# Two gated MLPs behind an attention block: longer buffers for the low parts of split operands

## Chip, cores, metric

One core of one Trainium2 chip. The metric is the device time of one launch in microseconds (us); the kernel before takes 986.37 us, the median of three runs (985.73 to 987.92).

## What is computed

```python
def _attn_ref(x, inducing):                       # x 1 x 12480 x 128, inducing 32 x 128
    h = mab(I, x)                                 # 32 inducing points attend to all rows
    return mab(x, h)                              # every row attends to the 32 results

def _moe_ref(x, w_in, w_out, alpha):              # w_in 128 x 2048, w_out 2048 x 128
    h = x @ w_in
    g = np.maximum(h, 0.0) + alpha * np.minimum(h, 0.0)
    return (g @ w_out).astype(np.float32)

def _moe2_ref(x, w_in, w_out):
    h = np.maximum(x @ w_in, 0.0)
    return (h * h @ w_out).astype(np.float32)
...
    x = attn_out.reshape(B * S, D)
    x = _moe_ref(x=x, **moe_kwargs)
    return _moe2_ref(x=x, **moe2_kwargs)
```

Rows: 12,480, cut into 30 row tiles of T = 416. The hidden width of 2,048 is cut into 16 chunks of 128.

## The kernel before

A first stage (some 100 us) loads and transposes x, runs the first attention, and brings the weights into shape. Then comes the main loop, a software pipeline over 480 chunk indices (30 row tiles x 16 chunks), written out step by step at the end of the function (lines 725 to 739).

Precision is kept by splitting: a float32 operand is stored as a high part in the reduced type float32r and a low part, the remainder, in the same type. A product then takes three matmuls with the same output bank (`three`, line 586): high by the weight's high part (L587), high by the weight's low part (L588), low by the weight's high part (L589). The parts are the moving operands, 128 partitions x 416 elements of 4 bytes, 1,664 bytes a partition.

In step s PE gets ten matmuls, in this order:
- L577 (`l1_a`, chunk s): `a_s`, the attention weights of the row tile s div 16, by `w1s`. ACT makes `g1h` of it (L581), DVE `g1l` (L583).
- L587, L588, L589 (`l2_a`, chunk s - 24): `y1h`, `y1h`, `y1l` by the second MLP's input weights w2i. ACT makes `r` (L619), DVE its square `sq` (L621), ACT `g2h` (L627), POOL `g2l` (L629).
- the same lines (`l1_b`, chunk s - 3): `g1h`, `g1h`, `g1l` by wo, summed into `y`.
- the same lines (`l2_b`, chunk s - 28): `g2h`, `g2h`, `g2l` by w2o, summed into `y`.

Where s - 3 is a multiple of 16, `l2_b` comes before `l1_b`. After the 16th chunk of a row tile `l1_b` calls `end_y1`: one more matmul (L604, `a_s` by `v_s`), then `y1h` (ACT, L606) and `y1l` (DVE, L608). Every fourth row tile four small matmuls for the next attention scores (L436) come in between. In the first 24 steps and the last 28 parts of the step are missing. PE works in program order; each other engine works through its own queue, and semaphores say when a tile may be read or overwritten.

Each kind of tile has a ring of buffers, taken in turn: `g1h`, `g1l`, `g2h`, `g2l` four each, `y1h`, `y1l` two each, `a_s` five. The buffers of a ring lie one behind the other in SBUF. As 1,664 is 6.5 x 256, neighbours in a ring begin at two offsets within 256 bytes in turn:

```
ring    first buffer at byte   start within 256 bytes, and who has which
g1h     170432                 192, 64, 192, 64   main loop: chunk even 192, odd 64
g1l     177088                 192, 64, 192, 64   main loop: chunk even 192, odd 64
g2h     183744                 192, 64, 192, 64   chunk even 192, odd 64
g2l     190400                 192, 64, 192, 64   chunk even 192, odd 64
y1h     197056                 192, 64            row tile even 192, odd 64
y1l     200384                 192, 64            row tile even 192, odd 64
a_s     131648                 64, 192, 64, 192, 64   row tile mod 5 is 2 or 4: 192, else 64
```

The weights' blocks all begin at 160 within 256 bytes (`v_s` at 32). As g1 has chunk s - 3 and g2 chunk s - 28, an even step has g1 at 64 and g2 at 192, an odd step g1 at 192 and g2 at 64. (For the first 20 chunks g1 uses the rings of g1 and g2 in turn.) In the trace, step 256 begins at 520.67 us, step 264 at 535.96, step 272 at 550.95, step 280 at 566.14 and step 288 at 581.13. Steps 256 to 271 have `a_s` of row tile 16 (at 64), steps 272 to 287 of row tile 17 (at 192); steps 248 to 263 have y1 of row tile 14 (at 192), steps 264 to 279 of row tile 15 (at 64), steps 280 to 295 of row tile 16 (at 192).

Of the kernel before, what the change touches and what calls it, by code (L numbers as in the profile page):

```python
# [10 lines left out]
F32R = mybir.dt.float32r  # L11
# [7 lines left out]
T = 416  # L19
# [9 lines left out]
def attention_then_two_mlps(ctx: ExitStack, tc, x, inducing, w_in, w_out, alpha, w2_in, w2_out, out):  # L29
# [7 lines left out]
    P = 128  # L37
# [531 lines left out]
    wk = ctx.enter_context(tc.tile_pool(name="wk", bufs=1))  # L569
# [3 lines left out]
    def l1_a(i, other_bank):  # L573
        t, c = divmod(i, NCH)
        b = h2_bank() if other_bank else h1_bank()
        a = a_s[t]
        nc.tensor.matmul(b[:, :T], w1s[: a.shape[0], c * P : (c + 1) * P], a, start=True, stop=True)  # L577

        tag = "g2" if i < EARLY and i % 2 else "g1"
        hi = wk.tile([P, T], F32R, name="g1h", tag=tag + "h", bufs=4)  # L580
        nc.scalar.activation(hi, b[:, :T], AF.Relu)  # L581
        lo = wk.tile([P, T], F32R, name="g1l", tag=tag + "l", bufs=4)
        nc.vector.scalar_tensor_tensor(lo, b[:, :T], 0.0, f32(hi), op0=ALU.max, op1=ALU.subtract)  # L583
        g1[i] = hi, lo

# [5 lines left out]
    def l1_b(i):  # L591
        t, c = divmod(i, NCH)
        if c == 0:
            y1_cur[t] = y1_bank() if t != 1 else y2_bank()
        b = y1_cur[t][:, :T]
        hi, lo = g1.pop(i)
        three(b, wo_hi[:, c, :], wo_lo[:, c, :], hi, lo, c == 0, False)
        if c == NCH - 1 and t:
            end_y1(t)

    def end_y1(t):
        b = y1_cur.pop(t)[:, :T]
        a = a_s.pop(t)
        nc.tensor.matmul(b, v_s[: a.shape[0]], a, start=False, stop=True)  # L604
        hi = wk.tile([P, T], F32R, name="y1h", tag="y1h", bufs=2)
        nc.scalar.copy(hi, b)  # L606
        lo = wk.tile([P, T], F32R, name="y1l", tag="y1l", bufs=2)
        nc.vector.tensor_tensor(lo, b, f32(hi), op=ALU.subtract)  # L608
        y1_split[t] = hi, lo

# [13 lines left out]
    def l2_split(i):  # L624
        sq = rr.pop(i)
        hi = wk.tile([P, T], F32R, name="g2h", tag="g2h", bufs=4)
        nc.scalar.copy(hi, sq)  # L627
        lo = wk.tile([P, T], F32R, name="g2l", tag="g2l", bufs=4)
        (nc.vector if i >= total - LAG2 else nc.gpsimd).tensor_tensor(lo, sq, f32(hi), op=ALU.subtract)  # L629
        g2[i] = hi, lo  # L630

# [54 lines left out]
    at(19, copy_u)  # L686
    at(20, step_v)
    at(22, end_y1, 0)
    for tiles in groups[1:]:
        for k, v in enumerate(second_attention(tiles)):  # L690
# [34 lines left out]
    for s in range(total + LAG2 + LAG2B + 4):  # L725
        if s < total:
            l1_a(s, s < LAG2 and s % 2)
        if 0 <= s - LAG2 < total:
            l2_a(s - LAG2)
        if 0 <= s - LAG2 - 1 < total:  # L730
            l2_split(s - LAG2 - 1)

        ends = [(l1_b, i) for i in l1_b_at.get(s, [])]
        if 0 <= s - LAG2 - LAG2B < total:
            ends.insert(0 if ends and ends[0][1] % NCH == 0 else len(ends), (l2_b, s - LAG2 - LAG2B))
        for f, i in ends:
            f(i)
        for f in plan.pop(s, []):
            f()
# [30 lines left out]
```

## Time and profile before

| | |
|---|---|
| runs | 987.92, 985.73, 986.37 us; median 986.37 |
| the profiled execution | 985.42 us, its span 983.6 us, 1.8 us lie around the span |
| mean granted TensorE clock | 0.997 |
| busy: PE, PE's weight loads, ACT, DVE, POOL | 965.0, 936.8, 768.5, 683.1, 555.1 us |
| instructions: PE, ACT, DVE, POOL | 5341, 1600, 1203, 518 |

A matmul's duration runs from its start to its modelled end and covers more than its turn on the array: the matmuls overlap, and the next one starts some 187 ns after the one before. The time that a step takes is read from the starts of the same line in consecutive steps; the timeline gives them to 0.01 us.

### The profile page before, as it was taken

What the parts mean: (1) busy time and instruction counts of PE and PEld (TensorE: products, weight loads), DVE (VectorE), ACT (ScalarE), POOL (GpSimd) and SP (SyncE); (2) the same over time, 40 slices, a digit from 0 to 9 for tenths busy, and PEclk for the clock granted to TensorE, in tenths of its full rate; (3) what the DMA queues carried; (4) which work ended last, traced back from release to release, by engine and by line L of the source; (5) the groups of instructions that cost most, each with busy time, mean ns of one, the idle gap of its engine ahead of it and who ended that gap; (6) DMA issues with size and microseconds to landing.
All of it is one profiled execution on the core that took longest, in us unless ns stands there. A gap on an engine that the chain in (4) does not pass through costs nothing.

```text
span 983.6 us, 16078 instructions
## 1 busy us (share of the span) xinstructions
PE 965.0 (98%) x5341; PEld 936.8 (95%) x5341; DVE 683.1 (69%) x1203; ACT 768.5 (78%) x1600; POOL 555.1 (56%) x518
## 2 busy tenths in 40 slices
PE   8889999999999999999999999999999999999997
PEld 6578999999999999999999999999999999999997
DVE  5788876667766677666776667766677666766677
ACT  5789887778877777777787777877778777787776
POOL 2358765555655556555565555655556555565530
PEclk9999999999999999999999999999999999999999
DMA  9431001000010000100001000010001000010001
GB/s 329 147 101 55 10 11 34 10 10 10 15 30 10 10 9 18 27 10 10 10 21 25 10 9 10 23 23 10 9 9 30 16 10 10 10 27 1 10 9 19
DMA packets 66356, 28.42 MB, mean 29 GB/s; under 512 B 54224, under 2 KB 62176, under 8 KB 66272
## 3 DMA queue, kind: packets, MB, share of 16 engines
q1 hardware_dynamic: 66272, 27.39, 11.3%
q8 instruction: 42, 0.69, 0.3%
q14 instruction: 42, 0.34, 0.1%
HBM read 14.80 MB, written 6.39 MB: 22 GB/s over the span
## 4 chain that ended last, share of the span: by engine, by line
PE 94%; DVE 2%; ACT 2%; DMA 1%; issue 0%; POOL 0%; SPq 0%; ACTq 0%; DVEq 0%
PE y L589 18%; PE y L588 18%; PE y L587 18%; PE h L587 9%; PE h L589 9%; PE h L588 9%; PE h L577 9%; PE h L248 1%; PE ms L260 1%; PE ms L436 1%; PE y L604 1%; ACT g1h L581 1%; PE y L321 1%; DMA xg<-in_x_dram 0%; DVE g1l L583 0%
## 5 line engine op out<-in xcount | busy, mean ns | idle before, releaser
L629 POOL TENSOR_TENSOR g2l<-sq,g2h 128x416 fp32r<-128x416 f32 x456 | 495.9, 1088 | 343.9 <-ACT g2h L627 244.2
L583 DVE SCALAR_TENSOR_TENSOR g1l<-h,g1h 128x416 fp32r<-128x416 f32 x480 | 282.7, 590 | 220.9 <-ACT g1h L581 216.5
L581 ACT ACTIVATE g1h<-h 128x416 fp32r<-128x416 f32 x480 | 248.7, 519 | 131.6 <-PE h L577 128.6
L621 DVE TENSOR_TENSOR sq<-h,r 128x416 f32<-128x416 f32 x480 | 283.6, 591 | 52.3 <-ACT r L619 4.9
L619 ACT ACTIVATE r<-h 128x416 f32<-128x416 f32 x480 | 249.4, 520 | 53.9 <-PE h L589 8.5
L627 ACT CAST g2h<-sq 128x416 fp32r<-128x416 f32 x480 | 255.4, 532 | 3.2 <-DVE sq L621 3.1
L577 PE MATMUL h<-a_s,w1s 128*128 128x416 f32 (+1 forms) x480 | 170.0, 355 | 4.5 <-DVE g1l L583 2.8
L589 PE MATMUL y<-g2l,w2o_hi 128*128 128x416 f32 x480 | 168.7, 351 | 0.3 <-POOL g2l L629 0.3
L587 PE MATMUL h<-y1h,w2i_hi 128*128 128x416 f32 x480 | 168.2, 350 | 0.2
L589 PE MATMUL y<-g1l,wo_hi 128*128 128x416 f32 x480 | 168.3, 351 | 0.0
L589 PE MATMUL h<-y1l,w2i_hi 128*128 128x416 f32 x480 | 167.9, 350 | 0.2 <-DVE y1l L608 0.2
L588 PE MATMUL h<-y1h,w2i_lo 128*128 128x416 f32 x480 | 168.0, 350 | 0.0
L588 PE MATMUL y<-g2h,w2o_lo 128*128 128x416 f32 x480 | 167.8, 350 | 0.0
L588 PE MATMUL y<-g1h,wo_lo 128*128 128x416 f32 x480 | 167.8, 350 | 0.0
L587 PE MATMUL y<-g1h,wo_hi 128*128 128x416 f32 x480 | 167.5, 349 | 0.0
L587 PE MATMUL y<-g2h,w2o_hi 128*128 128x416 f32 x480 | 167.5, 349 | 0.0
L577 PEld LDWEIGHTS h<-a_s,w1s 128*128 128x128 f32 (+1 forms) x480 | 90.1, 188 | 12.5 <-DVE g1l L583 6.1
L587 PEld LDWEIGHTS h<-y1h,w2i_hi 128*128 128x128 f32 x480 | 90.0, 188 | 3.1 <-DVE sq L621 1.7
L587 PEld LDWEIGHTS y<-g1h,wo_hi 128*128 128x128 f32 x480 | 90.3, 188 | 1.0 <-issue 0.5
L589 PEld LDWEIGHTS y<-g2l,w2o_hi 128*128 128x128 f32 x480 | 90.1, 188 | 1.2 <-POOL g2l L629 0.7
L589 PEld LDWEIGHTS h<-y1l,w2i_hi 128*128 128x128 f32 x480 | 90.0, 188 | 0.7 <-DVE y1l L608 0.5
L588 PEld LDWEIGHTS y<-g1h,wo_lo 128*128 128x128 f32 x480 | 90.2, 188 | 0.4
(121 smaller groups left out, 749.8 us busy)
## 6 DMA issues: line engine op xcount, KB each, us to landing
out_dram<-o SPq DMA_DIRECT2D x120, 52.0 KB, 1.9
xg<-in_x_dram SPq DMA_DIRECT2D x10, 512.0 KB, 8.4
raw<-in_moe_w_in_dram SPq DMA_DIRECT2D x8, 512.0 KB, 6.4
raw<-in_moe_w_out_dram SPq DMA_DIRECT2D x8, 512.0 KB, 4.1
a_s<-a_hi SPq DMA_DIRECT2D x58, 52.0 KB, 1.9
a_s<-a_lo SPq DMA_DIRECT2D x58, 52.0 KB, 1.9
xg<-in_x_dram SPq DMA_DIRECT2D x4, 256.0 KB, 3.8
xg<-in_x_dram SPq DMA_DIRECT2D x1, 96.0 KB, 5.8
```

The lines of the kernel that those rows point to most:

```text
L248: nc.tensor.transpose(b[:, k * p : (k + 1) * p], x_t[g][:p, i, k, :], ident[:p, :p])
L260: nc.tensor.matmul(b[i * M : (i + 1) * M, :n], indT, xT[:, t0 : t0 + n], start=True, stop=True, tile_position=(0, i * M),)
L577: nc.tensor.matmul(b[:, :T], w1s[: a.shape[0], c * P : (c + 1) * P], a, start=True, stop=True)
L581: nc.scalar.activation(hi, b[:, :T], AF.Relu)
L583: nc.vector.scalar_tensor_tensor(lo, b[:, :T], 0.0, f32(hi), op0=ALU.max, op1=ALU.subtract)
L587: nc.tensor.matmul(b, w_hi, hi, start=start, stop=False)
L588: nc.tensor.matmul(b, w_lo, hi, start=False, stop=False)
L589: nc.tensor.matmul(b, w_hi, lo, start=False, stop=stop)
L619: nc.scalar.activation(r, b, AF.Relu)
L621: nc.vector.tensor_tensor(sq, b, r, op=ALU.mult)
L627: nc.scalar.copy(hi, sq)
L629: (nc.vector if i >= total - LAG2 else nc.gpsimd).tensor_tensor(lo, sq, f32(hi), op=ALU.subtract)
```

## The change

The three rings of low parts get tiles that are 32 elements longer, of which the first 416 are used. A buffer is then 1,792 = 7 x 256 bytes long, and all buffers of `g1l`, `g2l` and `y1l` begin 192 bytes past a multiple of 256. The rings of four grow by 512 bytes, that of two by 256; what lies behind them moves by 512, 1,024 or 1,280 bytes. All other tiles keep their offset within 256 bytes, the high parts and `a_s` with the two offsets in turn among them. The last buffer ends at byte 216,640 of a partition (215,360 before).

```diff
@@ -579,7 +579,7 @@
         hi = wk.tile([P, T], F32R, name="g1h", tag=tag + "h", bufs=4)
         nc.scalar.activation(hi, b[:, :T], AF.Relu)
-        lo = wk.tile([P, T], F32R, name="g1l", tag=tag + "l", bufs=4)
+        lo = wk.tile([P, T + 32], F32R, name="g1l", tag=tag + "l", bufs=4)[:, :T]
         nc.vector.scalar_tensor_tensor(lo, b[:, :T], 0.0, f32(hi), op0=ALU.max, op1=ALU.subtract)
@@ -604,7 +604,7 @@
         hi = wk.tile([P, T], F32R, name="y1h", tag="y1h", bufs=2)
         nc.scalar.copy(hi, b)
-        lo = wk.tile([P, T], F32R, name="y1l", tag="y1l", bufs=2)
+        lo = wk.tile([P, T + 32], F32R, name="y1l", tag="y1l", bufs=2)[:, :T]
         nc.vector.tensor_tensor(lo, b, f32(hi), op=ALU.subtract)
@@ -625,7 +625,7 @@
         hi = wk.tile([P, T], F32R, name="g2h", tag="g2h", bufs=4)
         nc.scalar.copy(hi, sq)
-        lo = wk.tile([P, T], F32R, name="g2l", tag="g2l", bufs=4)
+        lo = wk.tile([P, T + 32], F32R, name="g2l", tag="g2l", bufs=4)[:, :T]
         (nc.vector if i >= total - LAG2 else nc.gpsimd).tensor_tensor(lo, sq, f32(hi), op=ALU.subtract)
```

## Rows read from the trace of the kernel before

**Rows 1.** The page: busy time and share of the engines, and the chain by engine.
```profile
PE 965.0 (98%) x5341; PEld 936.8 (95%) x5341; DVE 683.1 (69%) x1203; ACT 768.5 (78%) x1600; POOL 555.1 (56%) x518
...
PE 94%; DVE 2%; ACT 2%; DMA 1%; issue 0%; POOL 0%; SPq 0%; ACTq 0%; DVEq 0%
```

**Rows 2.** Windows: stretch, length, busy of PE, PEld, DVE, ACT, POOL, clock, DMA.
```profile
300.00:500.00 200.00, 200.00 (x1073) 197.32 (x1072) 137.16 (x237) 157.22 (x325) 116.53 (x108) 1.00 0.07 13
```

**Rows 3.** Groups by line, 300 to 500 us: count, busy, mean ns, idle before.
```profile
L629 POOL TENSOR_TENSOR g2l<-sq,g2h 128x416 fp32r<-128x416 f32 x105 | 114.0, 1086 | 82.9 <-ACT g2h L627 59.3 <-PE y L589 23.6
...
L583 DVE SCALAR_TENSOR_TENSOR g1l<-h,g1h 128x416 fp32r<-128x416 f32 x105 | 62.0, 590 | 50.7 <-ACT g1h L581 49.5
```

**Rows 4.** Timeline of PE, 520 to 582 us: start, duration (us); L577 begins a step.
```profile
520.67 0.35 PE L577 MATMUL h<-a_s,w1s 128*128 128x416 f32 x1
...
524.41 0.35 PE L577 MATMUL h<-a_s,w1s 128*128 128x416 f32 x1
...
525.73 0.35 PE L604 MATMUL y<-a_s,v_s 128*128 128x416 f32 x1
...
526.50 0.35 PE L577 MATMUL h<-a_s,w1s 128*128 128x416 f32 x1
...
532.21 0.35 PE L577 MATMUL h<-a_s,w1s 128*128 128x416 f32 x1
...
535.96 0.35 PE L577 MATMUL h<-a_s,w1s 128*128 128x416 f32 x1
...
537.83 0.35 PE L577 MATMUL h<-a_s,w1s 128*128 128x416 f32 x1
...
539.71 0.35 PE L577 MATMUL h<-a_s,w1s 128*128 128x416 f32 x1
...
541.57 0.35 PE L577 MATMUL h<-a_s,w1s 128*128 128x416 f32 x1
...
543.45 0.35 PE L577 MATMUL h<-a_s,w1s 128*128 128x416 f32 x1
...
545.32 0.35 PE L577 MATMUL h<-a_s,w1s 128*128 128x416 f32 x1
...
547.20 0.35 PE L577 MATMUL h<-a_s,w1s 128*128 128x416 f32 x1
...
549.07 0.35 PE L577 MATMUL h<-a_s,w1s 128*128 128x416 f32 x1
...
550.95 0.35 PE L577 MATMUL h<-a_s,w1s 128*128 128x416 f32 x1
...
566.14 0.35 PE L577 MATMUL h<-a_s,w1s 128*128 128x416 f32 x1
...
581.13 0.35 PE L577 MATMUL h<-a_s,w1s 128*128 128x416 f32 x1
```

**Rows 5.** PE's groups by line in the odd step 265, 537.81 to 539.69 us.
```profile
L588 PE MATMUL h<-y1h,w2i_lo 128*128 128x416 f32 x1 | 0.4, 353 | 0.0
L587 PE MATMUL h<-y1h,w2i_hi 128*128 128x416 f32 x1 | 0.3, 350 | 0.0
...
L577 PE MATMUL h<-a_s,w1s 128*128 128x416 f32 x1 | 0.3, 348 | 0.0
L589 PE MATMUL h<-y1l,w2i_hi 128*128 128x416 f32 x1 | 0.3, 348 | 0.0
```

**Rows 6.** PE's groups by line in the even step 282, 569.88 to 571.75 us.
```profile
L589 PE MATMUL y<-g1l,wo_hi 128*128 128x416 f32 x1 | 0.4, 353 | 0.0
L588 PE MATMUL y<-g1h,wo_lo 128*128 128x416 f32 x1 | 0.3, 350 | 0.0
L577 PE MATMUL h<-a_s,w1s 128*128 128x416 f32 x1 | 0.3, 349 | 0.0
```

**Rows 7.** PE's groups by line in the even step 264, 535.94 to 537.81 us.
```profile
L589 PE MATMUL y<-g1l,wo_hi 128*128 128x416 f32 x1 | 0.3, 347 | 0.0
```

**Rows 8.** PE's groups by line in step 260, 528.38 to 530.29 us.
```profile
L587 PE MATMUL y<-g2h,w2o_hi 128*128 128x416 f32 x1 | 0.4, 355 | 0.0
```

## The prediction

> **What bounds the kernel.** I read the page's busy shares and its chain first: TensorE (PE) is busy for 98% of the 983.6 us and makes 94% of the chain that ended last [rows 1]. The windows by stage say where: in the stretch from 300 to 500 us PE is busy for all 200.00 us at a granted clock of 1.00, which is the 2.4 GHz level [rows 2]. So in the main loop nothing but the distance from one matmul's start to the next sets the time. The writers of the low parts are far from that: in those 200 us POOL works 114.0 us on `g2l` and is idle 82.9 us ahead of it, DVE 62.0 us on `g1l` with 50.7 us idle [rows 3].
>
> The starts of L577, one per step of ten matmuls, show that steps are not equally long. From 535.96 to 550.95 us even and odd steps alternate: the four even ones take 7.47 us together (1.8675 each), the four odd ones 7.52 us (1.880 each). From 566.14 to 581.13 us eight steps take 14.99 us, 1.874 each, and so do the two from 520.67 to 524.41 us, 1.87 each [rows 4].
>
> **Which matmuls slip.** The mark is the duration. In an odd step of the first stretch `a_s`, `y1h` by w2i_hi and `y1h` by w2i_lo take 348, 350 and 353 ns, and `y1l` after them 348 [rows 5]. In a step of the second stretch it is `g1h` by wo_lo and `g1l` that show 350 and 353 ns, and `a_s` has the plain 349 [rows 6]. In the even steps of the first stretch `g1l` shows 347 [rows 7]. Laid beside the table of offsets, this has one reading. In the first stretch `a_s` and all y1 tiles lie at 64 (buffers of row tiles 16 and 15). An odd step then runs 64 64 64 64 | 192 192 192 | 64 64 64, and slips at its third tile and at its tenth, the third 64 after each change from 192. The even step after it begins inside a run of 64s that has paid already, and its first seven tiles cost nothing more. In the second stretch `a_s` and y1 lie at 192, and each step has one run of three 64s (g1 in even steps, g2 in odd ones): one slip. Around 520 us `a_s` is at 64 and y1 at 192; a single 64 between 192s adds nothing to 1.87 us. So **a run of moving operands at 64 pays once, at its third tile, whether that is a low tile or a high one**. The price: two slips make 1.880 out of 1.8675, one slip 1.874 (14.99/8), so 6.3 ns by either.
>
> **The change part by part.** Nothing is added or removed on any queue: no instruction, DMA or wait. Ten buffers grow by 128 bytes. Later tiles move by 512, 1,024 or 1,280 bytes, all multiples of 256, and keep their offsets; their first use lies behind the first stage's last reads as before, price nothing. The writers of the lows write at 192 in every step instead of every second; both offsets are in the means of [rows 3], and the idle time there covers a difference. Without that cover a longer write would show as PE waiting for `g1l` or `g2l`.
>
> What is left is the order of offsets in PE's 4,830 matmuls of the main loop, laid out from the code (480 steps of ten, and 30 of L604). Before: 82 runs of one 64, none of two, 519 of three or more (255 of three, 123 of four, 141 of six to eleven). After, with all lows at 192: 162 of one, **583 of two** (the highs of one triple), 138 of three or more (136 are `a_s` and two `y1h`, all at 64).
> - Removed: 519 x 6.3 ns = 3.27 us.
> - Kept: 138 x 6.3 ns = 0.87 us.
> - New: 583 x the price of a run of two, which the trace doesn't show. Lower bound 0, as for the run of one [rows 4]; a gain below the no-slip step is excluded because no context gives a step under 1.8675. Upper bound 6.3 ns, the full slip, 3.67 us. I take 1 ns, because the nearest row is the second tile of a longer run, 350 ns where 349 is plain [rows 5, 6], and the tile that paid the rest will no longer be at 64. That is 0.58 us.
>
> Sum: -3.27 + 0.87 + 0.58 = **-1.82 us**. The profiled execution took 985.42 us, so 983.60; the median of the runs shown is 986.37, 0.95 above it, and there the change gives **984.55 us**, 0.18% less. A measurement of this kernel tells about 0.2% (1.97 us) from no change, so the forecast lies just inside. Own range of this case: with 0 and with 2.5 ns for a run of two it is 984.0 to 985.4; about 0.9 us lower still if the disturbed steps below vanish.
>
> **Rivals.**
> *A. A run of two pays the whole slip.* Place: the second `g1h` and `g2h` matmul of each step, and `y1h` where it is at 64. For it: a slip may be owed from the entry and only show two tiles later. Against: the run of one owes nothing. Price 583 x 6.3 = 3.67 us, net +1.27 us, **987.6 us**. It decides above 4.1 ns per run, where 583 runs eat the 2.40 us.
>
> *B. A disturbed state lasts, slower than before.* From 526.50 to 532.21 us three steps take 5.71 us, 1.903 each, 30 ns over their neighbours [rows 4], and in them nearly every matmul is long, up to 355 ns for `g2h` at 192 [rows 8]. It begins behind L604, which ends a row tile, and where `a_s` is at 64 and y1 at 192 it lasts for three steps; I count 29 such steps, 0.9 us. What ends it is a step with a run of four 64s, and the change takes those runs away there. If it then lasts through all steps of that context (3/10 of 480, 144), that costs 144 x 30 ns = 4.3 us, 3.4 more than now: -1.82 + 3.4 = +1.6, **988.0 us**; if it spreads to half of all steps, 990.9. It decides from some 90 disturbed steps on. For it: after the change offsets alternate more often everywhere. Against: single 64s elsewhere don't start it.
>
> *C. Only the lows' offset counts.* Every slip goes, with the disturbed steps: -3.27 - 0.9, **982.2 us**; with the disturbed steps left, 983.1. Against: in [rows 5] the 353 ns stand at a high tile.
>
> *D. The change doesn't touch what makes the slips*, for instance PSUM banks or weights of odd chunks, which alternate with the same parity: 986.4 us. Against: which matmul slips changes with the buffers of `a_s` and y1 at the same parity [rows 5, 6]. The Trainium skill's page "SBUF — State Buffer" (SBUF: two separate sides) would stand behind this rival: it says that engines conflict only at the port pair that VectorE and GpSimd share and that TensorE waits for nobody, so an address could not matter; by it the sum is 0. The trace does not agree: steps with the same instructions differ by 13 ns with the offsets alone.
>
> **Numbers.** Chances: forecast 0.45 (nearly half of it beyond 0.2%, by the cheap end of a run of two or the vanished disturbed steps), A 0.2, B 0.17, C 0.1, D 0.08. Faster by over 0.2%: two fifths to half of the forecast's 0.45, plus C and a little for slips that I read too small, 0.34. Slower by over 0.2%: most of B and the top of A, 0.17. Within: 0.49. The range reaches from 983.0 (C with the disturbed steps left) to 988.4 (A, and B in its one context); B spread further and the low end of C are left out.
>
> **What would show it.** Right: steps with `a_s` and y1 at 192 (and those with only one of them at 64) fall from 1.874 to about 1.869 us; with both at 64 each step shows 1.874, its 353 ns at `y1h` by w2i_lo in even and odd steps; the whole-run means of `g1l` and `g2l` fall to 349 ns, while that of `y1h` by w2i_lo does not fall. A: the steps show 1.880, with long durations at or behind the second `g1h` and `g2h`. B: many steps at 1.90. Wrong altogether: slips that keep their places, or PE idle ahead of L587 to L589 behind DVE or POOL.

## The result, and the profile after

The changed kernel takes 999.98 us (median of 4 runs, 998.36 to 1001.33) against 986.15 us; the ratio is 1.0138 (95% interval 1.0123 to 1.0153). That is 13.8 us slower, outside the range forecast. All times here and below are of executions with a mean granted clock of 0.94 or more; two executions of `all64` (clock 0.557 and 0.752) and one of `all192` (0.848) are left out.

The page of the changed kernel, whose profiled execution took 1001.33 us, answers to [rows 1] with its first and last line; between them stand the two writers of low parts, over the whole run:

```profile
PE 980.9 (98%) x5341; PEld 941.0 (94%) x5341; DVE 684.1 (68%) x1203; ACT 769.2 (77%) x1600; POOL 555.1 (56%) x518
...
PE 94%; DVE 2%; ACT 2%; DMA 1%; issue 1%; SPq 0%; ACTq 0%; DVEq 0%
...
L629 POOL TENSOR_TENSOR g2l<-sq,g2h 128x416 fp32r<-128x416 f32 x456 | 496.5, 1089 | 357.3 <-ACT g2h L627 303.7
L583 DVE SCALAR_TENSOR_TENSOR g1l<-h,g1h 128x416 fp32r<-128x416 f32 x480 | 282.8, 590 | 229.7 <-ACT g1h L581 224.5
```

PE is still the chain. The same instructions ran in the same numbers, POOL and DVE write their lows in 1,089 and 590 ns as before, and both wait longer for ACT (303.7 and 224.5 us in all, 244.2 and 216.5 before), which waits for PE. PE alone became slower, without being idle. The windows view of the stretch that answers to [rows 2] says by how much:

```profile
300.00:500.00 200.00, 200.00 (x1056) 194.71 (x1055) 134.04 (x230) 154.36 (x319) 113.87 (x106) 1.00 0.07 13
```

In 200 us that PE fills at a granted clock of 1.00 it starts 1,056 matmuls instead of 1,073, 1.6% fewer. Over the main loop of some 870 us that is about the whole loss.

The timeline of PE gives the lengths of steps (L577 begins one) in three contexts, beside those of [rows 4]: from 529.22 us steps 256 and 257, from 544.62 steps 264 to 271, from 575.29 steps 280 to 287.

```profile
529.22 0.35 PE L577 MATMUL h<-a_s,w1s 128*128 128x416 f32 x1
...
533.01 0.35 PE L577 MATMUL h<-a_s,w1s 128*128 128x416 f32 x1
...
544.62 0.35 PE L577 MATMUL h<-a_s,w1s 128*128 128x416 f32 x1
546.51 0.35 PE L577 MATMUL h<-a_s,w1s 128*128 128x416 f32 x1
548.39 0.35 PE L577 MATMUL h<-a_s,w1s 128*128 128x416 f32 x1
...
559.77 0.35 PE L577 MATMUL h<-a_s,w1s 128*128 128x416 f32 x1
...
575.29 0.35 PE L577 MATMUL h<-a_s,w1s 128*128 128x416 f32 x1
...
590.71 0.35 PE L577 MATMUL h<-a_s,w1s 128*128 128x416 f32 x1
```

| context | before, us a step | after |
|---|---|---|
| `a_s` 64, y1 192 (steps 256, 257) | 1.870 | 1.895 |
| both 64 (steps 264 to 271) | 1.874 | 15.15/8 = 1.894 |
| both 192 (steps 280 to 287) | 1.874 | 15.42/8 = 1.928 |

The worst context is the one with the fewest operands at 64: only the two highs of one triple. The groups of step 282 there, 579.13 to 581.06 us (mean duration in ns behind the comma), beside [rows 6]:

```profile
L577 PE MATMUL h<-a_s,w1s 128*128 128x416 f32 x1 | 0.4, 354 | 0.0
L587 PE MATMUL h<-y1h,w2i_hi 128*128 128x416 f32 x1 | 0.4, 354 | 0.0
L589 PE MATMUL h<-y1l,w2i_hi 128*128 128x416 f32 x1 | 0.4, 354 | 0.0
...
L587 PE MATMUL y<-g1h,wo_hi 128*128 128x416 f32 x1 | 0.4, 353 | 0.0
L588 PE MATMUL y<-g1h,wo_lo 128*128 128x416 f32 x1 | 0.4, 351 | 0.0
```

It is not the two at 64 that are longest (353 and 351 ns), but all eight at 192 are long, 354 or 355 ns: `a_s` shows 354 where it had 349. The time is lost far from the operands that the forecast priced.

### The profile page after: what moved, and what is told of

Same layout as the page of the kernel before. It is cut to its first block, busy times and chain, and to the rows that moved or that the text cites. A ratio compares the mean times of both kernels' runs of the same rounds, so it can differ in the third digit from the quotient of the medians.

```text
span 999.6 us, 16078 instructions
## 1 busy us (share of the span) xinstructions
PE 980.9 (98%) x5341; PEld 941.0 (94%) x5341; DVE 684.1 (68%) x1203; ACT 769.2 (77%) x1600; POOL 555.1 (56%) x518
## 4 chain that ended last, share of the span: by engine, by line
PE 94%; DVE 2%; ACT 2%; DMA 1%; issue 1%; SPq 0%; ACTq 0%; DVEq 0%
PE y L589 18%; PE y L587 18%; PE y L588 18%; PE h L587 9%; PE h L589 9%; PE h L588 9%; PE h L577 9%; PE h L248 1%; PE ms L260 1%; PE ms L436 1%; PE y L604 1%; DMA xg<-in_x_dram 1%; ACT g1h L581 1%; PE y L321 1%; DVE g1l L583 0%
## 5 line engine op out<-in xcount | busy, mean ns | idle before, releaser
L629 POOL TENSOR_TENSOR g2l<-sq,g2h 128x416 fp32r<-128x416 f32 x456 | 496.5, 1089 | 357.3 <-ACT g2h L627 303.7
L583 DVE SCALAR_TENSOR_TENSOR g1l<-h,g1h 128x416 fp32r<-128x416 f32 x480 | 282.8, 590 | 229.7 <-ACT g1h L581 224.5
L577 PE MATMUL h<-a_s,w1s 128*128 128x416 f32 (+1 forms) x480 | 172.0, 359 | 4.5 <-DVE g1l L583 2.8
L577 PEld LDWEIGHTS h<-a_s,w1s 128*128 128x128 f32 (+1 forms) x480 | 90.3, 189 | 13.9 <-DVE g1l L583 6.6
L588 PEld LDWEIGHTS y<-g2h,w2o_lo 128*128 128x128 f32 x480 | 90.0, 188 | 2.0
L588 PEld LDWEIGHTS h<-y1h,w2i_lo 128*128 128x128 f32 x480 | 90.2, 188 | 1.7
```

The source lines that it names most:

```text
L588: nc.tensor.matmul(b, w_lo, hi, start=False, stop=False)
```

## The experiments

After the result there were two theories. **M**, a slow mode with a memory: a run of exactly two operands at 64 throws PE into a mode in which each matmul with an operand at 192 takes one slip (6.7 ns) longer, 193.3 instead of 186.7 ns from start to start, until a run of three or more at 64 ends it. **T**, a toll without memory: each change of offset between neighbours costs, and the change made more changes. Each experiment's ratio stands against executions of the kernel before on the same chip (medians 986.59 to 986.72 us).

### One offset for all: `all192` and `all64`

All seven rings of moving operands get buffers of 1,792 bytes. For 192 the tile ahead of the `a_s` ring is longer too:

```diff
-        hi = wk.tile([P, T], F32R, name="g1h", tag=tag + "h", bufs=4)
+        hi = wk.tile([P, T + 32], F32R, name="g1h", tag=tag + "h", bufs=4)[:, :T]
...
-        a_s[t] = att.tile([P, T], F32R, name="a_s", tag="a_s", bufs=5)
+        a_s[t] = att.tile([P, T + 32], F32R, name="a_s", tag="a_s", bufs=5)[:, :T]
...
-        t = v["t"] = att.tile([P, T], F32, name="a2t", tag="a2t")
+        t = v["t"] = att.tile([P, T + 32], F32, name="a2t", tag="a2t")[:, :T]
```

Without the last hunk the rings all lie at 64.

> All seven rings of moving operands (g1, g2, y1, high and low, and a_s) 1,792 bytes long and at offset 192, so no matmul of the main loop has an operand at 64. Theory M (two modes: a run of exactly two operands at 64 throws PE into a slow mode in which an operand at 192 takes 193.3 ns instead of 186.7, and only a run of three or more at 64 ends it): no run of two ever comes, so if nothing else starts the slow mode every step is 1.867 us and the time is 985.4 - 3.3 - 0.9 = about 981 to 983 us. But L604, which began the disturbed steps of the kernel before, may start it too, and then nothing here ends it: 1.933 us a step from step 22 on, about 1012 us. Theory T (no memory: every change of offset between neighbouring matmuls costs, and the change made more of them): no changes, 981 to 983 us.

> The same rings all at offset 64. Theory M: one long run of 64s pays once and then stays at 186.7 ns, and L604 did not disturb the contexts at 64: 1.867 us a step, 981 to 983 us, faster than both kernels by 0.3 to 0.5%. Theory T: the same time, as nothing changes offset. A rival in which 64 itself is the costly offset: longer than before.

Measured: `all192` 983.53 us, ratio 0.9966 (0.9953 to 0.9979); `all64` 983.3 us, 0.9961 (0.9945 to 0.9977). Both beat both kernels. Offsets that differ cost, and neither offset is slow by itself. M and T both allow it.

### The mirror: `lows64`

The lows lie at 64 instead of 192, and the highs alternate as before:

```diff
-        lo = wk.tile([P, T], F32R, name="g1l", tag=tag + "l", bufs=4)
+        lo = wk.tile([P, T + 32], F32R, name="g1l", tag=tag + "l", bufs=4)[:, 32:]
...
```

(and likewise `y1l`, `g2l`).

> The mirror of the change: the three rings of low parts 1,792 bytes long, but all at offset 64 instead of 192; the highs alternate as before. Theory M: triples are 64 64 64 or 192 192 64; the single 64s cost nothing, runs of two come only where g2l at 64 meets a_s at 64 before a y1h at 192 (82 times, against 583 in the changed kernel), so 985 to 990 us. Theory T: as many changes of offset between neighbours as in the changed kernel, so about as slow as that, 996 to 1000 us.

Measured: 986.28 us, ratio 0.9993 (0.9983 to 1.0002). The offsets change between neighbours 1,632 times, in the changed kernel 1,765 and before 1,200 times, and it costs nothing: T falls. Triples of two 192 and a single 64 are harmless where triples of two 64 and a single 192 are not.

### Offset of the operand, or its distance to the weights: `wshift` and `after_wshift`

The weights move by 128 bytes, in the kernel before and in the changed one:

```diff
-    w1s = keep_tile("w1s", [P, DFF], F32R)
+    w1s = keep_tile("w1s", [P, DFF + 32], F32R)[:, 32:]
...
-    al = keep_tile("al", [P, NCH])
+    al = keep_tile("al", [P, NCH + 32])[:, :NCH]
```

> The kernel before with all weight blocks 128 bytes further on: they begin at 32 instead of 160 within 256 bytes; the moving operands keep their offsets. If the slip comes from moving reads against weight reads, what counts is the distance between the two: 64 and 192 change parts, and the 193 ns matmul is the third in each run of operands at 192 (in steps with a_s and y1 at 192 the long duration moves from g1l or g2l to another tile). If the offset of the moving operand alone counts, the same tiles slip as before. The time is near that of before by either, within 5 us, as runs of two operands at 192 do not occur.

Measured: 985.56 us, ratio 0.9984 (0.9971 to 0.9997). The groups of its step 282 (570.34 to 572.22 us, both `a_s` and y1 at 192), beside [rows 6]:

```profile
L588 PE MATMUL h<-y1h,w2i_lo 128*128 128x416 f32 x1 | 0.4, 353 | 0.0
L587 PE MATMUL h<-y1h,w2i_hi 128*128 128x416 f32 x1 | 0.3, 350 | 0.0
...
L589 PE MATMUL y<-g1l,wo_hi 128*128 128x416 f32 x1 | 0.3, 349 | 0.0
L577 PE MATMUL h<-a_s,w1s 128*128 128x416 f32 x1 | 0.3, 348 | 0.0
```

348, 350, 353 now stand at `a_s`, `y1h`, `y1h`, all at 192, and `g1l` at 64 is plain. So 64 and 192 have changed parts: **what counts is the distance between the moving operand and the weights** within 256 bytes, not the operand's own offset. Two distances occur: operand less weights is 32 for the plain ones, and 160 for those that slip (called the paying distance below), in both kernels. The 1.1 us that it gains are about the 0.9 us that I had put down to the disturbed steps, and its trace has none of them: L604's `v_s` lies at 32, where the other weights lie now too.

> The changed kernel with all weight blocks 128 bytes further on (at 32 instead of 160 within 256 bytes); moving operands exactly as in the changed kernel. Theory R (what counts is the distance between the moving operand and the weights that are read at the same time, so 192 now has the part that 64 had): the triples become three of the paying offset, or two of the free one and a single paying one, the pattern of the kernel with lows at 64, which took 986.3: 984 to 988 us, and no 193 ns matmuls one after the other. Theory O (the offset of the moving operand alone counts): 999 to 1001 us as the changed kernel.

Measured: 987.03 us, ratio 1.0003 (0.9992 to 1.0013): the changed kernel with its weights 128 bytes further on has none of the 13.8 us. Its timeline, steps 280 to 287:

```profile
568.56 0.35 PE L577 MATMUL h<-a_s,w1s 128*128 128x416 f32 x1
...
583.54 0.35 PE L577 MATMUL h<-a_s,w1s 128*128 128x416 f32 x1
```

14.98/8 = 1.873 us a step instead of 1.928, with the moving operands where they were. The theory of the operand's own offset (999 to 1001) falls.

### Does the slow mode last? `all192_y1h`

As `all192`, but the ring of `y1h` keeps its 1,664 bytes. So the only operands at 64 are two `y1h` in each step of the odd row tiles of y1.

> All rings at 192 except y1h, whose two buffers alternate as before: in odd row tiles of y1 every step has one run of exactly two operands at 64 (y1h, y1h) with eight at 192 between, in even row tiles there is none at all. Theory M (a run of two starts the slow mode, and nothing but a run of three ends it): from the first odd row tile on all operands at 192 take 193 ns, in the even row tiles too, where nothing is at 64: 1.92 to 1.933 us a step, about 1008 to 1012 us. Theory L (the slow mode is kept up only by runs of two that come again within ten matmuls): odd row tiles at 1.92, even ones at 1.867 us a step, about 995 us. Theory N (a run of two alone starts nothing; it takes more frequent changes): 1.867 to 1.875 us in all, 982 to 985 us.

Measured: 1007.47 us, ratio 1.0215 (1.0194 to 1.0235). Its timeline around step 288, with the small matmuls of the attention scores (L436):

```profile
579.37 0.35 PE L577 MATMUL h<-a_s,w1s 128*128 128x416 f32 x1
...
594.84 0.35 PE L577 MATMUL h<-a_s,w1s 128*128 128x416 f32 x1
...
596.85 0.91 PE L436 MATMUL ms<-xT,hT 128*32 128x416 f32 x8
...
603.59 0.35 PE L577 MATMUL h<-a_s,w1s 128*128 128x416 f32 x1
...
611.06 0.35 PE L577 MATMUL h<-a_s,w1s 128*128 128x416 f32 x1
```

Steps 280 to 287 have no operand at 64 at all (row tile 16 of y1 is even), and yet they take 15.47/8 = 1.934 us each, ten slips a step. The last operand at 64 lies one to eight steps back. Behind L436, steps 292 to 295 take 7.47/4 = 1.8675 each, and the 1.927 us a step of the odd row tile come back with the next run of two. So M is right on the memory, L and N fall. M was incomplete on the way out: an interruption by L436 ended the mode here too.

Nor does M's rule on what ends the mode hold in every context. In the changed kernel with `a_s` and y1 at 64, step 265 (from 546.51 us) ends with the run of two `g2h`, `g2h` and a `g2l` at 192, and step 266 begins with the run of three `a_s`, `y1h`, `y1h`. By M the three end the mode, but step 266 is the long one, 1.92 us against 1.88, and its `y1l`, right behind the three, takes 355 ns, that of step 265 only 348:

```profile
548.39 0.35 PE L577 MATMUL h<-a_s,w1s 128*128 128x416 f32 x1
550.31 0.35 PE L577 MATMUL h<-a_s,w1s 128*128 128x416 f32 x1
```

```profile
L589 PE MATMUL h<-y1l,w2i_hi 128*128 128x416 f32 x1 | 0.4, 355 | 0.0
```

So a run of three that comes one operand behind a run of two did not end it. In the kernel before, the runs of three in steps 259 and 260 do not end the disturbed stretch from 526.50 to 532.21 us either [rows 4]; the four at 64 behind them do. The two levels, the memory and the part of the distance are shown; M's rule for start and end fits the steps with both at 192 and those of `all192_y1h`, and in general it is open.

### The three rings one by one

One hunk of the change each.

> The change for the ring of g1l alone (its first buffers in the g2l ring too are as before). Runs of two at 64 come in even steps (g1h, g1h), ended by the three of g2 in the odd step: 337 runs of two. Theory M: slow from there to the next run of three, some 1,900 operands at 192 at 193 ns, 10 to 13 us more than before, 996 to 999 us. A rival in which each of the three rings brings its part in proportion to its runs of two (337 of 583): 8 us, 994 us.

> The change for the ring of y1l alone: 104 runs of two at 64 (y1h, y1h, where a_s is at 192), each ended soon by the three of g1 or g2 at 64, and 404 runs of three. Theory M: some 230 operands at 192 in the slow mode, 2 us more than before, 988 to 989 us. In proportion to the runs of two (104 of 583): 2.5 us, 989 us; a rival in which y1l is harmless alone: 986 to 987 us.

> The change for the rings of g2l alone: 219 runs of two at 64 (g2h, g2h in odd steps where neither a_s nor y1 prolongs them), ended by the three of g1 in the next even step. Theory M: some 720 operands at 192 in the slow mode, 4 to 5 us more than before, 990 to 992 us. In proportion to the runs of two (219 of 583): 5 us. If the three rings' costs simply added up, g2l would bring less than nothing, as g1l (10.5 us) and y1l (4.6) make 15.1 of 13.5 already: then 985 us.

| hunk | buffers of 1,792 bytes | us | ratio | M had said |
|---|---|---|---|---|
| `g1l` | `g1l` and `g2l` | 997.04 | 1.0109 (1.0089 to 1.0129) | 996 to 999 |
| `g2l` | `g2l` | 991.85 | 1.0054 (1.0036 to 1.0072) | 990 to 992 |
| `y1l` | `y1l` | 991.23 | 1.0050 (1.0034 to 1.0066) | 988 to 989 |

The hunk of `g1l` does more than its name and its expectation say. Of the first 20 chunks every second one takes its `g1l` from the ring of `g2l`, and all buffers of a ring have the length of its longest tile. So in `g1l_only` the buffers of `g2l` are 1,792 bytes long too (they begin at 190912, 192704, 194496 and 196288) and all lie at 192: the kernel is the changed one without `y1l`. No three of g2 at 64 end the mode there, and its steps 280 to 287, with `a_s` and y1 at 192, take 15.40/8 = 1.925 us, about as long as in the changed kernel (1.928):

```profile
572.55 0.35 PE L577 MATMUL h<-a_s,w1s 128*128 128x416 f32 x1
...
587.95 0.35 PE L577 MATMUL h<-a_s,w1s 128*128 128x416 f32 x1
```

The 337 runs of two in its expectation are those of these addresses; `g1l` alone was not run. So `g1l` and `g2l` together cost 10.5 us, `g2l` alone 5.2, `y1l` alone 4.6, and all three 13.8: `y1l` adds some 3 us to the other two. That it adds less than alone would fit a mode that is on or off, as a slow stretch can't be made slow again; no run tests that. M hit two of the three and was too low on `y1l`. There, with `a_s` at 192 and y1 at 64, the three g1 of an even step again come one operand behind the run of two `y1h`, and the g2 behind them are long all the same, which M had not counted (step 278, from 567.26 us):

```profile
L587 PE MATMUL y<-g2h,w2o_hi 128*128 128x416 f32 x1 | 0.4, 355 | 0.0
```

For `g2l` a cost in proportion to the runs of two came to the same 5 us, so that run doesn't tell the two apart.

### The better version once more

> The kernel with all rings at 192 once more, on another chip if it falls so, to tell its gain from the scatter: theory M gives 3.2 to 4.2 us less than before, a ratio of 0.9957 to 0.9968, and 1.867 us in every plain step.

> The kernel with all rings at 64 once more beside it: theory M gives the same time as with all at 192, within 0.1%, and 1.867 us in every plain step. A rival: one of the two uniform offsets keeps a cost of its own.

Measured: `all64` 980.97 us, ratio 0.9942 (0.9928 to 0.9955); `all192` 984.3 us, 0.9974 (0.9962 to 0.9986). In its two series `all64` is 0.4 and 0.6% faster than the kernel before. Its page, its windows view and its timeline over steps 280 to 287, one after the other:

```profile
PE 963.2 (98%) x5341; PEld 937.1 (96%) x5341; DVE 683.2 (70%) x1203; ACT 769.2 (78%) x1600; POOL 554.7 (57%) x518
```

```profile
300.00:500.00 200.00, 200.00 (x1078) 198.04 (x1077) 138.15 (x239) 157.82 (x326) 117.12 (x109) 1.00 0.07 13
```

```profile
565.05 0.35 PE L577 MATMUL h<-a_s,w1s 128*128 128x416 f32 x1
...
579.98 0.35 PE L577 MATMUL h<-a_s,w1s 128*128 128x416 f32 x1
```

1,078 matmuls in 200 us, and 14.93/8 = 1.866 us a step. `all192` did not come out equal in this series, as M had said it would (in the first the two were equal, 983.5 and 983.3 us). Its timeline says why (ten steps from 196.49, ten from 232.18 us):

```profile
196.49 0.35 PE L577 MATMUL h<-a_s,w1s 128*128 128x416 f32 x1
...
215.82 0.35 PE L577 MATMUL h<-a_s,w1s 128*128 128x416 f32 x1
...
232.18 0.35 PE L577 MATMUL h<-a_s,w1s 128*128 128x416 f32 x1
...
250.84 0.35 PE L577 MATMUL h<-a_s,w1s 128*128 128x416 f32 x1
```

1.933 us a step at first, 1.866 later: the slow mode, with no main-loop operand at 64 to start it. It runs from step 33, behind an L436, up to the L436 at step 96, some 60 steps x 67 ns = 4.0 us; the two profiled executions, 985.85 and 982.24 us, lie 3.6 us apart. In the trace of `all192` from the first series the same mode is short: 1.93 us a step over the four from 104.65 us, which are steps 36 to 39, and 1.8675 over the four from 114.32.

```profile
104.65 0.35 PE L577 MATMUL h<-a_s,w1s 128*128 128x416 f32 x1
...
112.37 0.35 PE L577 MATMUL h<-a_s,w1s 128*128 128x416 f32 x1
114.32 0.35 PE L577 MATMUL h<-a_s,w1s 128*128 128x416 f32 x1
...
121.79 0.35 PE L577 MATMUL h<-a_s,w1s 128*128 128x416 f32 x1
```

So its length differs from execution to execution. What starts it there is open: with all operands at one offset the layout has no run of two, and the later L436 do not start it. In the second series' trace of `all64` no step is slow.

## Why the prediction was wrong

- **PE's matmul pitch is the bound, and nothing else moves: right.** Busy times, the chain and the writers' durations stand.
- **A run of 64s pays once, at its third tile: right as far as it went.** All-64 steps take 1.866 us and the 3.3 us of slips are there to be had (980.97 and 983.3 us; with the same two terms gone, case C had come to 982.2). The reading left out that the distance to the weights is what matters, which `wshift` shows.
- **The step that failed is the price of a run of two**, "Upper bound 6.3 ns, the full slip". From the result, 13.8 = -3.27 + 0.87 + 583 x, so x is 28 ns, 28 times the 1 ns taken and over four times the bound. The bound was taken from within a run (350 for 349 ns, one slip at most), on the unspoken premise that the 192s after a run are plain again. In the trace of before they were, but for the disturbed steps, and by the operands' own offsets no run there had two tiles. What the runs showed in its place: the operands behind the run pay, one slip each, 1.934 us a step against 1.8675.
- **The disturbed steps may have been the missing row.** Set against the weights of the matmul behind it, the `g1l` ahead of L604 meets `v_s` at 32 and so does not lie at the paying distance, and where y1 lies at 192 the two `g1h` before it are a run of two. In the timeline of before, disturbed steps follow L604 after each of the 14 odd row tiles from 1 to 27, where that is so, and after none of the 14 even ones from 2 to 28. In the window from 525.50 us the long durations begin at that `g1l`, one matmul ahead of L604:

```profile
L589 PE MATMUL y<-g1l,wo_hi 128*128 128x416 f32 x1 | 0.4, 356 | 0.0
L587 PE MATMUL y<-g2h,w2o_hi 128*128 128x416 f32 x1 | 0.4, 354 | 0.0
...
L588 PE MATMUL y<-g1h,wo_lo 128*128 128x416 f32 x1 | 0.3, 350 | 0.0
```

  `wshift`, where `v_s` lies like the other weights, has no such steps. No run moves `v_s` alone, so this is argued and not shown.
- **Rival A, the full slip for each run**: 987.6, too small for the same reason.
- **Rival B, a lasting disturbed state: the right mechanism, with the wrong start and size.** I had seen steps of 1.903 us with long matmuls at 192 [rows 4, 8] and that a longer run of 64s ends them. But I let it begin at L604 only, hold in one context of four, and cost 30 ns a step. It begins without L604 too, costs up to 61 ns a step (1.928 - 1.867), and lengthens the steps of all four contexts: the eight from 559.77 to 575.29 us, with `a_s` at 192 and y1 at 64, take 15.52 us, before 15.19 [rows 4]. At 988 to 991 us and a chance of 0.17 it was under-priced on both counts. That nearly every matmul of a disturbed step is long, those at 192 among them, spoke for a state and against a toll, and should have set the upper end of the range.
- **Rival D falls**: kernels with the same main-loop instructions and lengths differ from 980.97 to 1007.47 us by addresses alone. With it falls what I drew there from the Trainium skill's page "SBUF — State Buffer" (SBUF: two separate sides), that an address could not matter. The page's rule itself, on engines that wait for one another, is neither borne out nor refuted: which reads meet none of the runs shows.
- **The marks.** The steps with both at 192 went to 1.928 us instead of 1.869, and those with both at 64 to 1.894 instead of 1.874. "B: many steps at 1.90" is what came.

## What to carry to other kernels

Where the matmul pitch is the bound, as here, try giving all moving operands of the stream the same distance to its weights within 256 bytes, by buffer lengths that are multiples of 256 for all rings at once: it brought 0.3 to 0.6% here, and aligning half of them was worse than aligning none. Look at the addresses that come out, too, as tiles that share a ring share its buffer length. A cost that was read inside one pattern of addresses bounds nothing for a pattern that the trace does not contain, least of all where some steps already show a state that outlives its cause. And where PE is the bound, compare the starts of the same line from step to step: PE was 98% busy in the kernel before, in the changed one and in the fastest one alike.

## What the runs showed that was not expected

- PE's pitch has two levels at the same granted clock of 1.00 and with the same work: 1.8675 and 1.934 us for ten matmuls, 186.7 and 193.3 ns each. The upper one holds by itself over eight steps and more without any operand at the other offset (`all192_y1h`).
- With `a_s` and y1 at 192 a run of two operands at the paying distance puts PE into it and keeps it there, and an interruption by L436 ended it (`all192_y1h`). A run of three ended it in some places and not where it came one operand behind a run of two (step 266 of the changed kernel, step 278 of `y1l_only`). Why two, and how reads of weights and operands meet in the memory, none of the runs shows.
- One uniform distance gave a steady main loop (`all64`), while with the other the slow mode held for the steps from 33 to 95 in one trace and from step 33 to step 40 in another (`all192`).
